# Attention and two MLPs on one core: batch bits, value loads, first issues, clamps and output stores rearranged

## The chip, the cores and the metric

The kernel runs on 1 core of one Trainium2 chip. The metric is device time in microseconds (us), the median of several runs. One execution was also taken by the hardware profiler; its rows are quoted below. Engine names are those of the profile: PE is TensorE's matmul, PEld its weight load, DVE VectorE, ACT ScalarE, POOL GpSimd, SP SyncE; SPq and ACTq are the instructions by which SyncE and ScalarE issue DMAs.

## The reference, cut to what matters

```python
# q, k, v: (4, 8, 768, 48) float32; beta: (4, 8, 768); w_in (384, 2048) and w_out (2048, 384) twice, float64
k_n = k / (norm(k) + 1e-6)
for t in range(768):                                   # per batch b and head h
    y[:, :, t] = einsum('bhd,bhde->bhe', q[:, :, t], state)
    v_old = einsum('bhde,bhd->bhe', state, k_n[:, :, t])
    state += beta_t * einsum('bhd,bhe->bhde', k_n[:, :, t], v[:, :, t] - v_old)
x = y.transpose(0, 2, 1, 3).reshape(3072, 384)
h = x @ w_in;  x = ((a0 + a1 h + a2 h^2 + a3 h^3) / (1 + |b0||h| + |b1|h^2 + 1e-6)) @ w_out   # first MLP
h = x @ w_in2; out = (h * tanh(softplus(h))) @ w_out2                                          # second MLP
```

## The kernel before, in words

**Stages.** The sequence of 768 is cut into 24 steps of 32 positions (`C`), four steps to a group (`GU`), six groups (`NG`). A group is 4 batches x 128 positions = 512 tokens. For each group the attention makes X (512 tokens x 384, kept as a high and a low half), the first MLP turns X into a new X, the second MLP turns that into the output.

**Attention.** The 32 pairs of batch and head lie in four lanes of 32 partitions, eight pairs (`M`) in each. `norms` loads the keys (`load_k`, four DMAs per step) and takes their lengths; `prepare` normalises keys, transposes keys and queries (`load_q`, four DMAs) on TensorE and forms the products within the step; `inverse` solves the triangular systems of four steps at once by 30 pairs of elementwise operations, on GpSimd for groups 1 to 5, on VectorE for group 0; `step` runs the serial recurrence: values (`load_v`, line 239, eight DMAs of 24 KB per step), a swap of key halves between lanes by two DMAs (`swap`), then TensorE, VectorE and ScalarE by turns. In `setup` the first group's keys are loaded by SyncE and ScalarE, beta by eight DMAs of GpSimd.

**Weights.** They arrive as 64-bit floats. `Weights.plan` turns a block of 384 KB into a high and a low 32-bit half in `win` or `wout` and writes it to a scratch `wd` in HBM, from which later groups fetch it. A block passes through: load (`get`, seven DMAs for the first w_in, else one) into one of five `raw` buffers; `clamp` of the upper words (line 624); `fold` or `scale` and `sign`; `shift`; `tail`; `hi`; then the low half, by TensorE and ScalarE (`lo_mm`, `lo_copy`) or by GpSimd (`lo`). The letters of `kind` choose: with "v" the clamp is VectorE's and writes a PSUM bank, and the low half is GpSimd's; without it the clamp is GpSimd's. The first twelve pairs of blocks of the first MLP have no letter; four pairs of the first and four of the second have "v"; the last twelve pairs have "mv".

**MLPs.** A unit (`plan_unit`) is one block of 128 hidden columns for one group: nine matmuls `up` (line 760), activations on ScalarE, VectorE and GpSimd, nine matmuls `down` (line 766) into three output tiles `o0` to `o2`. 16 units make a group of one MLP, 192 units in all. From the second group on the weights of a unit are fetched from `wd` by two DMAs (line 753), into four slots each of `win` and `wout`.

**Output.** For the groups 0 to 4 of the second MLP the result stands by columns: VectorE transposes each tile into one of two buffers `ev` (line 832) and SyncE stores it by 16 DMAs of 16 KB (`store`, line 839), 48 per group. For the last group `down_rows` (line 775) gives rows of tokens in four tiles (`o0` to `o2`, `t0`), which are copied to `ev` (line 818) and stored by one DMA of 192 KB each (`store_rows`, line 847).

**What sets the order.** All work is recorded in a `Plan`: `add` takes an engine, a duration in ns, what is read and written, a due time and `early`; `dma` the same for a DMA, with the time that its issue takes on its queue. `order` works from these numbers which instruction each engine takes next: among those ready, the one with the least time to its due time, less `early`. `lead` gives `early` for attention work: for group 1 `NEAR`, 20 us. The result is a fixed order on each engine; SyncE, ScalarE, VectorE and GpSimd each take theirs strictly in turn. `run` also puts filler matmuls (`heat`, line 909) where the plan sees TensorE idle in the start up.

## Time and profile before

| | us |
|---|---|
| three runs | 1224.94, 1228.59, 1234.18; median 1228.59 |
| profiled execution, device time | 1236.0 |
| its span, first to last instruction | 1234.3 |
| mean granted clock of TensorE in it | 0.941 of 2.4 GHz |

The span is what the rows count, from 0 at the first instruction. The profiled execution is one run among the others, a little longer than their median.

### The profile page before, as it was taken

How to read it: one execution, taken by the hardware profiler on the slowest of the kernel's cores; microseconds unless marked ns; L12 is line 12 of the kernel's file. 1: busy time of each engine (PE TensorE's matmuls, PEld its weight loads, DVE VectorE, ACT ScalarE, POOL GpSimd, SP SyncE). 2: the span in 40 equal slices, each digit the busy share in tenths (PEclk: the TensorE clock that was granted, in tenths of full speed). 3: DMA queues.
4: the chain of work that ended last, by engine and by line, in shares of the span. 5: the costliest groups of instructions: out<-in, count | busy, mean ns of one | idle time of the engine just before them, and what ended most of it. 6: DMA issues, size and time to landing. Idle time of an engine off the chain costs nothing.

```text
span 1234.3 us, 32780 instructions
## 1 busy us (share of the span) xinstructions
PE 1070.5 (87%) x13510; PEld 855.5 (69%) x13510; DVE 654.6 (53%) x1088; ACT 617.3 (50%) x1087; POOL 553.5 (45%) x705
## 2 busy tenths in 40 slices
PE   5566799688878997999899998999986999999885
PEld 4444577466656786777778776887865788788775
DVE  4663389867657742248662357732263578721211
ACT  3334488734367751257752276832263588832211
POOL 5102169695236796726576035683043257600000
PEclk9877889898989998999999999999998999999988
DMA  5575683656763864464866565755536366767462
GB/s 126 121 204 134 211 249 123 208 185 194 218 181 89 251 178 117 117 173 109 234 172 172 128 169 133 227 160 145 154 95 185 94 175 188 190 184 193 121 200 62
DMA packets 201221, 202.80 MB, mean 164 GB/s; under 512 B 133968, under 2 KB 146768, under 8 KB 201072
## 3 DMA queue, kind: packets, MB, share of 16 engines
q1 hardware_dynamic: 198640, 200.22, 58.6%
q8 instruction: 106, 1.74, 0.6%
q10 hardware_dynamic: 2176, 0.39, 0.2%
q14 instruction: 43, 0.35, 0.1%
q0 software_dynamic: 256, 0.10, 0.0%
HBM read 168.40 MB, written 29.88 MB: 161 GB/s over the span
## 4 chain that ended last, share of the span: by engine, by line
PE 54%; SPq 15%; DMA 9%; DVE 7%; POOL 7%; ACT 5%; issue 3%; DVEq 0%; POOLq 0%; ACTq 0%
PE b_h L760 23%; PE b_o L766 20%; SPq L839 7%; DMA kn<-in_k_dram 3%; POOL xs L425 2%; PE b_t L531 2%; POOL tmp L419 2%; SPq L229 2%; PE b_t L510 2%; DMA wout<-wd 1%; PE b_o L775 1%; SPq L617 1%; PE b_t L496 1%; DMA wd<-x 1%; SPq L242 1%
## 5 line engine op out<-in xcount | busy, mean ns | idle before, releaser
L760 PE MATMUL b_h<-x,win 128*128 128x512 f32 x1620 | 416.8, 404 | 32.2 <-DMA win<-wd 14.2
L766 PE MATMUL b_o<-gh,wout 128*128 128x512 f32 x1476 | 378.1, 403 | 18.4 <-DMA wout<-wd 9.6
L760 PEld LDWEIGHTS b_h<-x,win 128*128 128x128 f32 x1620 | 306.7, 193 | 104.1 <-DVE ms L800 15.5
L766 PEld LDWEIGHTS b_o<-gh,wout 128*128 128x128 f32 x1476 | 279.2, 192 | 83.0 <-DMA wout<-wd 9.9
L811 DVE TENSOR_TENSOR gh<-mq,gh 128x512 fp32r<-128x512 f32 x96 | 75.6, 788 | 195.3 <-ACT mq L810 185.1
L798 POOL TENSOR_TENSOR mq<-mq,mr 128x512 f32<-128x512 f32 x96 | 124.1, 1292 | 110.0 <-ACT mr L796 104.4
L809 ACT ACTIVATE gh<-b_h 128x512 fp32r<-128x512 f32 x96 | 57.3, 597 | 214.2 <-PE b_h L760 207.9
L807 POOL TENSOR_TENSOR gh<-mq,gh 128x512 fp32r<-128x512 f32 x96 | 124.0, 1292 | 70.1 <-ACT gh L806 70.0
L799 DVE TENSOR_TENSOR ms<-ms,b_h 128x512 f32<-128x512 f32 x96 | 65.5, 682 | 59.1 <-ACT ms L797 56.9
L425 POOL TENSOR_TENSOR xs<-xs,tmp 128x30 f32<-128x30 f32 (+9 forms) x150 | 84.1, 561 | 11.8
L792 ACT ACTIVATE mq<-b_h 128x512 f32<-128x512 f32 x96 | 56.8, 592 | 62.3 <-PE b_h L760 60.3
L803 DVE SCALAR_TENSOR_TENSOR mq<-mq,b_r 128x512 f32<-128x512 f32 x96 | 65.6, 683 | 38.1 <-ACT b_r L802 34.7
L419 POOL TENSOR_TENSOR tmp<-xs 128x30 f32<-128x30 f32 (+9 forms) x150 | 79.1, 527 | 10.1
L797 ACT ACTIVATE ms<-b_h,ab 128x512 f32<-128x512 f32 x96 | 73.8, 769 | 8.5 <-PE b_h L760 8.1
L790 ACT ACTIVATE mr<-mq,cst 128x512 f32<-128x512 f32 x96 | 69.1, 720 | 16.8 <-POOL mq L798 16.6
L800 DVE SCALAR_TENSOR_TENSOR ms<-ms,ab,b_h 128x512 f32<-128x512 f32 x96 | 71.8, 748 | 3.2
L806 ACT CAST gh<-mq 128x512 fp32r<-128x512 f32 x96 | 58.9, 615 | 27.8 <-DVE mq L805 26.4
L804 DVE SCALAR_TENSOR_TENSOR b_r<-ms,ab,b_r 128x512 f32<-128x512 f32 x96 | 71.9, 749 | 0.0
L805 DVE SCALAR_TENSOR_TENSOR mq<-mq,b_r 128x512 f32<-128x512 f32 x96 | 65.8, 685 | 2.6
L794 POOL TENSOR_SCALAR mr<-mq,ab 128x512 f32<-128x512 f32 x48 | 37.1, 772 | 60.1 <-ACT mq L792 60.1
L802 ACT ACTIVATE b_r<-mr 128x512 f32<-128x512 f32 x96 | 57.7, 601 | 7.5 <-DVE mq L805 6.3
L810 ACT ACTIVATE mq<-b_h 128x512 f32<-128x512 f32 x96 | 56.9, 594 | 2.4 <-PE b_h L760 2.4
(168 smaller groups left out, 1311.4 us busy)
## 6 DMA issues: line engine op xcount, KB each, us to landing
win<-wd SPq DMA_DIRECT2D x164, 384.0 KB
wout<-wd SPq DMA_DIRECT2D x164, 384.0 KB
arena<-in_moe_w_out_dram SPq DMA_DIRECT2D x32, 384.0 KB
wd<-x SPq DMA_DIRECT2D x24, 384.0 KB
wd<-win SPq DMA_DIRECT2D x16, 384.0 KB
wd<-wout SPq DMA_DIRECT2D x16, 384.0 KB
arena<-in_moe_w_in_dram SPq DMA_DIRECT2D x16, 384.0 KB
v<-in_v_dram SPq DMA_DIRECT2D x192, 24.0 KB
```

The lines of the kernel that those rows point to most:

```text
L419: eng.tensor_tensor(out=tv, in0=row[:, j, j + 1:C].unsqueeze(1).to_broadcast([128, j, n]), in1=xs[:, 0:j, j:j + 1].to_broadcast([128, j, n ...
L425: eng.tensor_tensor(out=xs[:, 0:j, j + 1:C], in0=xs[:, 0:j, j + 1:C], in1=tv, op=ALU.add)
L760: nc.tensor.matmul(out=h, lhsT=win[:, a, j], rhs=x[:, c, slab[j]], start=n == 0, stop=n == 8)
L766: nc.tensor.matmul(out=self.banks[f"o{d}"], lhsT=wout[:, a, d], rhs=gh[:, c], start=first and j == 0, stop=last and j == 2,)
L790: act(out=r, in_=q, func=ACTF.Ln, bias=k["c"])
L797: p.add("ACT", 775, lambda: act(out=s, in_=h, func=ACTF.Identity, scale=k["a3"], bias=k["a2"]), [hb], [sb])
L798: p.add("POOL", 1335, lambda: P.tensor_tensor(out=q, in0=q, in1=r, op=ALU.mult), [rb], [qb])
L800: p.add("DVE", 750, lambda: V.scalar_tensor_tensor(out=s, in0=s, scalar=k["a1"], in1=h, op0=ALU.add, op1=ALU.mult), [hb], [sb])
L804: p.add("DVE", 750, lambda: V.scalar_tensor_tensor(out=rp, in0=s, scalar=k["a0"], in1=rp, op0=ALU.add, op1=ALU.mult), [sb], ["r"])
L807: p.add("POOL", 1320, lambda: P.tensor_tensor(out=gh[:, 1], in0=q, in1=gh[:, 0].bitcast(F32), op=ALU.subtract), [qb], [ghb])
L811: p.add("DVE", 755, lambda: V.tensor_tensor(out=gh[:, 1], in0=q, in1=gh[:, 0].bitcast(F32), op=ALU.subtract), [qb], [ghb])
L839: self.nc.sync.dma_start(out=self.out[row:row + 32, d * 128:(d + 1) * 128].rearrange("t (a c) -> a t c", c=32), in_=ev[:, 32 * n:32 * n + 32],
```

## The change

- **Lanes.** Lane e of the keys and queries held the batch 2 (e // 2) + e % 2; now it holds 2 (e % 2) + e // 2. The eight pairs of a lane's values and of beta then lie evenly in HBM, so that `load_v` needs four DMAs of 48 KB instead of eight of 24, and beta four. The rows of the output are permuted back in `store` and `store_rows`.
- **Issues.** In group 0 the queries and values are issued by ScalarE instead of SyncE.
- **Clamps.** All clamps are on GpSimd, in SBUF; the letter "v" becomes "p", which now chooses the low half on GpSimd alone.
- **Output.** Group 4 also uses `down_rows`. Each row tile is stored by four DMAs of 48 KB, tiles 0 and 2 by SyncE, 1 and 3 by ScalarE. There are three `ev` buffers, and `ms0` serves as a fourth. The stores of the groups 0 to 3 are due 20 `PACE` (84 us) after their unit instead of 7.5.
- **Numbers of the planner.** `NEAR` is 40 us; most durations given to the plan are new, so that the order of instructions changes on every engine.

```diff
-NEAR = 20000
+NEAR = 40000
...
-        vv = v.rearrange("b h s d -> (b h) s d").rearrange("(a c n r) s d -> r c a s n d", a=2, c=2, r=2)
+        vv = v.rearrange("b h s d -> (b h) s d").rearrange("(a m r) s d -> r a s m d", a=2, r=2)
-        self.kv = [kv[e // 2, e % 2] for e in range(4)]
+        self.kv = [kv[e % 2, e // 2] for e in range(4)]
-        self.vv = [[vv[1 - e // 2, e % 2, a] for a in range(2)] for e in range(4)]
+        self.vv = [vv[1 - e // 2, e % 2] for e in range(4)]
...
-    def load_v(self, u):
+    def load_v(self, u, engine=None):
         for e in range(4):
-            for a in range(2):
-                self.nc.sync.dma_start(
-                    out=self.v[u % self.NV][32 * e:32 * e + 32, 4 * a:4 * a + 4], in_=self.vv[e][a][C * u:C * u + C]
-                )
+            (engine or self.nc.sync).dma_start(out=self.v[u % self.NV][32 * e:32 * e + 32], in_=self.vv[e][C * u:C * u + C])
...
-            p.dma(4 * 450, 300, lambda: self.load_q(u), (), [qnb], early=lead(AHEADP, G))
+            p.dma(2250, 300, lambda: self.load_q(u, None if G else nc.scalar), (), [qnb], early=lead(AHEADP, G), engine="SP" if G else "ACT")
...
-        p.dma(8 * 400, 300, lambda: self.load_v(u), (), [vb], early=lead(AHEAD, G))
+        p.dma(2250, 300, lambda: self.load_v(u, None if G else nc.scalar), (), [vb], early=lead(AHEAD, G), engine="SP" if G else "ACT")
...
         def clamp():
-            (nc.vector if "v" in kind else nc.gpsimd).tensor_scalar(
-                out=at, in0=high.bitcast(F32), scalar1=self.MOST, scalar2=-self.MOST, op0=ALU.min, op1=ALU.max,
+            nc.gpsimd.tensor_scalar(
+                out=v, in0=high.bitcast(F32), scalar1=self.MOST, scalar2=-self.MOST, op0=ALU.min, op1=ALU.max,
             )
...
-        p.dma(380 if side or self.n else 2500, 384, get, (), [rawb])
-        if "v" in kind:
-            p.add("DVE", 520, clamp, [rawb], [here])
-        else:
-            p.add("POOL", 1490, clamp, [rawb], [here])
+        p.dma(430 if side or self.n else 3300, 384, get, (), [rawb])
+        p.add("POOL", 540, clamp, [rawb], [mb])
...
-        if m == 2 and G == NG - 1:
+        if m == 2 and G >= NG - 2:
...
-                ev, evb = self.ev[b_ % 2], f"ev{b_ % 2}"
+                ev, evb = (self.ev[b_], f"ev{b_}") if b_ < 3 else (self.s[0], "ms0")
...
-                p.dma(340, 200, lambda b_=b_, ev=ev: self.store_rows(G, b_, ev), [evb], ())
+                for c in range(self.B):
+                    eng = "ACT" if b_ % 2 else "SP"
+                    p.dma(500, 50, lambda b_=b_, ev=ev, c=c, eng=eng: self.store_rows(G, b_, ev, c, A if eng == "ACT" else nc.sync), [evb], (), engine=eng)
...
-                ev, evb = self.ev[d % 2], f"ev{d % 2}"
+                ev, evb = self.ev[d], f"ev{d}"
...
-                    p.dma(340, 40, lambda n=n, d=d, ev=ev: self.store(G, d, ev, n), [evb], (), due=due + (LAG + 4) * PACE)
+                    p.dma(590, 40, lambda n=n, d=d, ev=ev: self.store(G, d, ev, n), [evb], (), due=due + 20 * PACE)
...
-    def store_rows(self, G, b, ev):
-        row = (G * GU + b) * C
-        out = self.out.rearrange("(b s) d -> b s d", b=self.B)
-        self.nc.sync.dma_start(out=out[:, row:row + C], in_=ev[:, 0:384])
+    def store_rows(self, G, j, ev, b, engine):
+        row = (b % 2 * 2 + b // 2) * self.S + (G * GU + j) * C
+        engine.dma_start(out=self.out[row:row + C], in_=ev[32 * b:32 * b + 32, 0:384])
```

The order of the instructions, at three places. First SyncE's queue in the start up, behind the loads of the third block of w_in; `v` are values, `qn` queries, `kn` keys, `kns` swapped keys, `arena` the raw weights. Before:

```order
L621 DMA arena<-in_moe_w_in_dram 48x128
L610 DMA arena<-in_moe_w_out_dram 128x384
L242 DMA v_150<-in_v_dram 32x4x48 x8
L610 DMA arena<-in_moe_w_out_dram 128x384
L235 DMA qn_148<-in_q_dram 32x8x48 x4
L477 DMA kns_152<-kn_147 64x4x48
L478 DMA kns_152<-kn_147 64x4x48
L242 DMA v_151<-in_v_dram 32x4x48 x8
```

and in the changed kernel:

```order
L616 DMA arena<-in_moe_w_in_dram 48x128
L605 DMA arena<-in_moe_w_out_dram 128x384
L229 DMA kn_148<-in_k_dram 32x8x48 x4
L605 DMA arena<-in_moe_w_out_dram 128x384
L229 DMA kn_148<-in_k_dram 32x8x48 x4
L612 DMA arena<-in_moe_w_in_dram 48x2x128 x2
L612 DMA arena<-in_moe_w_in_dram 32x2x128
L615 DMA arena<-in_moe_w_in_dram 16x128
L616 DMA arena<-in_moe_w_in_dram 48x128
```

The values and queries are gone from here; the keys of group 1 and the loads of the next weights stand in their place. ScalarE's order at its start, in the changed kernel, where `sq` and `r` are the squares of the keys, and the kernel before has the same squares and no values or queries:

```order
L229 DMA kn_148<-in_k_dram 32x8x48 x8
L892 ACTIVATE minus<-ident_144 128x128
L241 DMA v_151<-in_v_dram 32x8x48 x4
L235 DMA qn_149<-in_q_dram 32x8x48 x4
L303 ACTIVATE sq_171<-kn_148 128x384
L303 ACTIVATE r_170<-kn_148 128x384
L241 DMA v_152<-in_v_dram 32x8x48 x4
L303 ACTIVATE sq_171<-kn_148 128x384
L303 ACTIVATE r_170<-kn_148 128x384
L624 ACTIVATE arena<-arena 128x384
L235 DMA qn_150<-in_q_dram 32x8x48 x4
```

Twelve of the moved issues stand before the last two squares, four more behind them. Second, SyncE's queue at the stores of the fourth group of the second MLP (`out_dram`), among the fetches of weights (`win`, `wout` from `wd`). Before:

```order
L753 DMA win_116<-wd_5_65 128x768
L753 DMA wout_122<-wd_3_63 128x768
L839 DMA out_dram<-ev_138 4x32x32 x16
L839 DMA out_dram<-ev_139 4x32x32 x16
L839 DMA out_dram<-ev_138 4x32x32 x16
L753 DMA win_117<-wd_6_66 128x768
L753 DMA wout_119<-wd_4_64 128x768
L753 DMA win_118<-wd_7_67 128x768
```

and in the changed kernel:

```order
L744 DMA win_117<-wd_6_66 128x768
L832 DMA out_dram<-ev_138 4x32x32 x7
L744 DMA wout_119<-wd_4_64 128x768
L832 DMA out_dram<-ev_138 4x32x32 x2
L744 DMA win_118<-wd_7_67 128x768
L832 DMA out_dram<-ev_138 4x32x32 x4
L744 DMA win_115<-wd_8_68 128x768
L832 DMA out_dram<-ev_138 4x32x32 x3
L744 DMA wout_120<-wd_5_65 128x768
L241 DMA v_151<-in_v_dram 32x8x48 x4
```

The 48 stores stood in one run; now they stand two to seven at a time between single fetches, and the values of a later step among them. Third, GpSimd among the first units of the first MLP: `mq` and `gh` are products and low halves of the units, `x` the low half of a weight block, `mr` a polynomial. Before:

```order
L794 TENSOR_SCALAR mr_130<-mq_126,ab 128x512
L798 TENSOR_TENSOR mq_126<-mq_126,mr_130 128x512
L807 TENSOR_TENSOR gh_134<-mq_124,gh_134 128x512
L798 TENSOR_TENSOR mq_123<-mq_123,mr_131 128x512
L807 TENSOR_TENSOR gh_135<-mq_125,gh_135 128x512
L382 TENSOR_TENSOR mb_164<-beta_t_146,mask_144 128x256
L653 TENSOR_TENSOR x_113<-arena,x_113 128x384
L794 TENSOR_SCALAR mr_132<-mq_124,ab 128x512
L807 TENSOR_TENSOR gh_136<-mq_126,gh_136 128x512
L798 TENSOR_TENSOR mq_124<-mq_124,mr_132 128x512
L653 TENSOR_TENSOR x_113<-arena,x_113 128x384
```

and in the changed kernel:

```order
L373 TENSOR_TENSOR kn_148<-kn_148,nrm_4_187 128x8x48 x3
L785 TENSOR_SCALAR mr_130<-mq_126,ab 128x512
L789 TENSOR_TENSOR mq_126<-mq_126,mr_130 128x512
L798 TENSOR_TENSOR gh_134<-mq_124,gh_134 128x512
L789 TENSOR_TENSOR mq_123<-mq_123,mr_131 128x512
L648 TENSOR_TENSOR x_113<-arena,x_113 128x384
L798 TENSOR_TENSOR gh_135<-mq_125,gh_135 128x512
L619 TENSOR_SCALAR arena<-arena 128x384
L785 TENSOR_SCALAR mr_132<-mq_124,ab 128x512
L789 TENSOR_TENSOR mq_124<-mq_124,mr_132 128x512
L798 TENSOR_TENSOR gh_136<-mq_126,gh_136 128x512
```

A clamp (`arena<-arena`) now stands between the units' instructions, ahead of the product of `mq_124`; before, no clamp stood among the units on this engine.

## Rows read from the trace of the kernel before

**Rows 1.** the page, busy time, share of the span and instructions of TensorE.

```profile
PE 1070.5 (87%) x13510; PEld 855.5 (69%) x13510; DVE 654.6 (53%) x1088; ACT 617.3 (50%) x1087; POOL 553.5 (45%) x705
```

**Rows 2.** stretches: length, busy time by engine, granted clock, DMA share, GB/s.

```profile
0.80:82.50 81.70, 46.49 (x851) 36.62 (x852) 51.30 (x124) 28.15 (x61) 21.24 (x47) 0.81 0.59 147
82.50:157.10 74.60, 48.33 (x1278) 34.86 (x1277) 29.60 (x59) 34.30 (x76) 13.52 (x19) 0.81 0.63 179
157.10:238.00 80.90, 74.56 (x495) 58.86 (x495) 73.82 (x125) 66.46 (x117) 60.63 (x58) 0.96 0.62 186
238.00:290.00 52.00, 37.81 (x194) 29.65 (x195) 36.67 (x61) 21.47 (x42) 47.86 (x78) 0.80 0.61 197
290.00:367.00 77.00, 64.37 (x1487) 50.04 (x1486) 50.95 (x93) 39.28 (x73) 20.25 (x20) 0.93 0.69 201
400.00:440.00 40.00, 37.08 (x308) 29.29 (x296) 31.43 (x49) 30.29 (x51) 29.77 (x38) 1.00 0.83 240
```

**Rows 3.** SyncE's queue in order of time, start up: start, us, issues.

```profile
18.22 4.22 SPq L242 DMA_DIRECT2D v<-in_v_dram  x8
...
22.96 1.92 SPq L235 DMA_DIRECT2D qn<-in_q_dram  x4
...
26.34 5.00 SPq L242 DMA_DIRECT2D v<-in_v_dram  x8
```

**Rows 4.** the chain that ended last, start up: start, us, what.

```profile
46.25 3.08 DMA qn<-in_q_dram
```

**Rows 5.** VectorE in order of time, the first inverse.

```profile
52.02 0.35 DVE L419 TENSOR_TENSOR tmp<-xs,b_o 128x184 f32<-128x184 f32 x1 [5.50 <-ACT xs L433]
```

**Rows 6.** line 242, SyncE's issues of values: duration ns min/median/max.

```profile
L242 SPq DMA_DIRECT2D v<-in_v_dram x40: 311/430/1613, 18.2 to 144.4; - x40
```

**Rows 7.** line 229, ScalarE's issues of keys: duration ns min/median/max.

```profile
L229 ACTq DMA_DIRECT2D kn<-in_k_dram x8: 317/436/472, 0.8 to 6.1; - x8
```

**Rows 8.** waits of TensorE: total us, times, longest.

```profile
PE b_h L760 <- DMA win<-wd: 14.2, 3, 8.3
...
PE b_o L766 <- DMA wout<-wd: 9.6, 4, 3.6
...
PE b_o L766 <- DVE ev L832: 4.6, 2, 2.7
...
PE b_o L775 <- DVE ev L832: 3.2, 1, 3.2
```

**Rows 9.** TensorE in order of time, two units right behind a wait.

```profile
936.73 4.18 PE L760 MATMUL b_h<-x,win 128*128 128x512 f32 x9 [8.28 <-DMA win<-wd]
...
1183.09 4.11 PE L760 MATMUL b_h<-x,win 128*128 128x512 f32 x9 [5.43 <-DMA win<-wd]
```

**Rows 10.** SyncE's queue, stores of the fourth group.

```profile
905.23 28.05 SPq L839 DMA_DIRECT2D out_dram<-ev  x48
```

**Rows 11.** clamps (line 624): busy us, mean ns, idle before by releaser.

```profile
L624 DVE TENSOR_SCALAR b_r<-arena 128x384 f32<-128x384 f32 x24 | 13.4, 560 | 0.7
...
L624 POOL TENSOR_SCALAR arena<-arena 128x384 f32<-128x384 f32 x24 | 12.9, 537 | 93.7 <-PE b_h L658 28.8 <-DMA kn<-in_k_dram 23.9 <-DMA arena<-in_moe_w_in_dram 17.7
...
L624 DVE TENSOR_SCALAR b_t<-arena 128x384 f32<-128x384 f32 x16 | 8.9, 559 | 8.0 <-DMA arena<-in_moe_w_in_dram 7.7
```

**Rows 12.** clamps on GpSimd: duration ns min/median/max, first and last start.

```profile
L624 POOL TENSOR_SCALAR arena<-arena x24: 518/528/713, 12.3 to 131.3; 128x384 f32<-128x384 f32 x24
```

**Rows 13.** TensorE, two units with column results and two with row results.

```profile
1140.24 2.20 PE L760 MATMUL b_h<-x,win 128*128 128x512 f32 x9
...
1144.32 2.20 PE L760 MATMUL b_h<-x,win 128*128 128x512 f32 x9
...
1189.12 2.24 PE L760 MATMUL b_h<-x,win 128*128 128x512 f32 x9
...
1193.31 2.24 PE L760 MATMUL b_h<-x,win 128*128 128x512 f32 x9
```

**Rows 14.** SyncE's queue, the last four stores.

```profile
1220.74 7.72 SPq L847 DMA_DIRECT2D out_dram<-ev  x4
```

71 lines of the change are left out of this document (34 added, 37 removed).

## The prediction

> **What bounds the kernel now.** I read the page first: TensorE is busy 87% of the span [rows 1], so nothing that TensorE hides is worth anything, and what can be won is the other 164 us (1234.3 - 1070.5) and the time that it ran at its lower clock. Then the stretches [rows 2], which show three regimes. Up to 157 us TensorE does set-up work, 46.5 of 81.7 us and 48.3 of 74.6, at a mean granted clock of 0.81, that is, part of the time at 1.2 GHz instead of 2.4. From 157 to 367 us it shares the time with the conversion of the second weights. From 400 us on it is nearly always busy. So I looked for what it waits for in each, in the list of waits, SyncE's queue and the chain.
>
> In the start up, SyncE is the late one. Its queue issues without a pause, and values, queries, values are issued one behind the other for 4.22 + 1.92 + 5.00 us [rows 3], all of which the chain lists, while the weight loads that the conversions wait for stand behind them. Then a query load, issued late, is on the chain for another 3.08 us [rows 4]; TensorE and ScalarE wait for it in their order, and VectorE's inverse stands still for 5.50 us because ScalarE has not reached the copy that it needs [rows 5].
>
> Later the waits of TensorE have one origin. At the end of a group of the second MLP, SyncE issues 48 stores, in the fourth group all in one row: 28.05 us [rows 10], 0.58 each, and the fetches of weights stand behind them. TensorE waits for fetched weights 14.2 + 9.6 us in seven places and for the two output tiles to be free 4.6 + 3.2 us in three [rows 8]. Right behind such a wait a unit's nine matmuls take 4.18 or 4.11 us [rows 9], against 2.04 in a steady unit (half of the 4.08 from one start to the next, 1144.32 - 1140.24 [rows 13]): the lower clock costs about 2 us per wait, in four places about 8.
>
> **The change part by part.** The sums are made against the profiled execution's own time, 1236.0 us (span 1234.3 and 1.7 around it). It lies 0.6% above the median of the three runs, 1228.59; at the end I scale by 1228.59 / 1236.0 = 0.994.
>
> *Start up.* 16 query issues and 16 value issues of the first group move to ScalarE's queue, and 16 more value issues disappear (32 become 16). That is 48 issues off SyncE. An issue has a median of 0.43 us [rows 6], 0.48 with the gap behind it (5.00 + 4.22 + 1.92 us for 20 [rows 3] are 0.56, with waits in them), so 23 us. On the chain I find 11.1 us of them [rows 3] and the pause of 5.5 [rows 5], 16.6. Against it: ScalarE pays 0.44 per issue [rows 7], and twelve issues stand ahead of the last two squares and four more ahead of the logarithm of the first norms. Part of this hides behind VectorE's reductions; I put the delay of that chain at 3.7 us (eight issues). Net 13. The other 16 issues lie beside ScalarE's slack, 28.2 us busy of 81.7 [rows 2]; each waits for a tile that was read long before in its order. If that cover were gone they would cost 7 us. Bounds: nothing gained (the DMA engines turn out late, or ScalarE gives back what SyncE wins) and 28.5 - 3.7 = 25 us (all 23 and the pause).
>
> On this the trace and a rule of the skill differ. SyncE's issue time is on the chain [rows 3], and the DMA engines are busy 0.59 and 0.63 of these stretches, against 0.83 in a later one [rows 2]. The Trainium skill, DMA: Bandwidth & Descriptors, section Issuing engines are not separate DMA queues, says that issuing from several engines saves only the issuing time, which is usually small beside the transfer. By the rows the term is 13 us, by that rule about none.
>
> *Clamps.* 40 clamps leave VectorE: 24 and 16 of 0.56 us [rows 11], 22.4 us. They go to GpSimd, where 24 like them take 0.537 [rows 11], 21.5 us more there. From 157 to 238 us VectorE is busy 73.8 of 80.9 and GpSimd 60.6; from 238 to 290 GpSimd is the late one, 47.9 of 52 [rows 2], with the inverse of the second group. In the new order four clamps stand inside that inverse, but six low halves instead of ten, at 1 us each: 2 us less. About ten conversions lie ahead of it on the chain, 5.6 us of clamps less on VectorE; 14 clamps more stand ahead on GpSimd, 7.5 us, in a stretch with 20.3 us to spare. I take 4 us gained, between 15 (two thirds of the 22.4) and a loss whose size depends on what a clamp waits for (third rival).
>
> The 24 clamps on GpSimd take 518 to 713 ns, with a median of 528 [rows 12]; with all 40 at the upper end it would be 7 us more, inside GpSimd's spare time. The Trainium skill, SBUF — State Buffer, section SBUF: two separate sides, says that VectorE and GpSimd share a port pair which one instruction holds to its end, so that the other stands. The rows up to 713 ns do not refute that. By that rule the four clamps inside the inverse would each stand for up to a whole VectorE operation of 0.55 us, and the term would be 2 us instead of 4.
>
> *Stores.* The 48 stores of each of the first four groups stay, with a new due time and a real price in the planner. In the new order at most seven follow each other (4.1 us), with fetches between. The queue then needs 48 x 0.58 + 14 fetches and 8 query issues at 0.43 [rows 6], 9.5, = 37 us for seven units, of 4.1 us each without attention work beside them; it falls behind by at most 9 us, and the fetches run four units, 16 us, ahead. The fifth group's 48 become 16, half of them on ScalarE, whose work there is two operations per unit. The third and fourth output tiles remove the waits for a free one. To be had: 14.2 + 9.6 + 4.6 + 3.2 + 8 = 39.6 us; I take 32, since some fetches will still come late. Bounds 0 and 39.6.
>
> *Tail.* The last store is issued at 1220.74 + 7.72 = 1228.5 us [rows 14], 5.8 us before the end. Now eight issues on each queue at 0.48 end near 1225.0 (ScalarE's start at 1221.1). Gain 3.5 at the same landing time; I take 5, because 48 KB land sooner than 192 (3.08 us [rows 4]). Bounds 3 and 8.
>
> *Fifth group by rows.* A unit with row results takes 4.19 us (1193.31 - 1189.12), one with column results 4.08 [rows 13]: 16 x 0.11 = 1.7 us lost. The halved value issues of later groups and of beta lie beside TensorE: nothing, and 3 us if a fetch waited behind them.
>
> Sum: 13 + 4 + 32 + 5 - 1.7 = 52.3. 1236.0 - 52.3 = 1183.7; times 0.994, 1177 us.
>
> **The rivals.**
> 1. The start up is not shortened: the transfers or the serial attention steps are late, not SyncE. For it: DMA shares near 0.6 with waits for landings between the issues [rows 4]. Against it: 0.83 is reached later [rows 2]. 13 us less: 1196.7, scaled 1190. This is also the sum by the skill's rule on issuing engines.
> 2. The stores do not do what the edit says: the queue issues in order, a fetch that waits for TensorE holds the stores behind it, they bunch up, and the fetches are late once more. Without the 32 us: 1215.7, scaled 1208. Against it: the new order lets no more than seven follow each other.
> 3. The other side: GpSimd is held up by late weights. A clamp waits for its raw weights at the head of GpSimd's queue, and products and low halves of the units, which TensorE needs, stand behind it. Price: on VectorE these 40 waited 0.7 + 8.0 us, 0.2 each; the 24 on GpSimd had 93.7 us of idle time before them, 3.9 each [rows 11]. I take the former, the same instructions with the same loads. GpSimd's spare time from 157 to 367 us is 20.3 + 4.1 + 56.8 = 81 us [rows 2]. At 3.9 each the 40 need 40 x 4.4 = 178, 97 over: 1177 + 4 + 97 = 1278. Slower than before from about 2.9 us each.
> 4. The new order, made with new costs everywhere, gives back elsewhere what the edits win: near 1228.
>
> **How the numbers follow.** Forecast 0.58 (own range 1152 to 1192), first rival 0.17, second 0.12, third 0.06, fourth 0.04, something else and slower 0.03. A measurement of this kernel tells about 1%, 12 us, from no change. The first three are faster by more than that: 0.87. Same: 0.05 (the fourth and a part of the other rest). Slower: 0.08 (the third, and what is left). Upper ends of all terms, 25 + 15 + 39.6 + 8 - 1.7 = 86, give 1143; the range starts at 1150, as not all can hold, and ends at 1212, with the second rival in it.
>
> **What would show it.** Right: the dense units of TensorE begin near 144 us instead of 157, where the second stretch of [rows 2] ends; no wait for fetched weights over 2 us at the ends of groups; the last store within 5 us of the last matmul. Wrong: SyncE idle before 150 us with weights landing no sooner (rival 1); fetches late behind stores (rival 2); clamps on GpSimd with long idle times before them between 157 and 290 us, and TensorE idle there for more than the present 20.5 us, 80.9 - 74.6 and 52.0 - 37.8 [rows 2] (rival 3).

## The result and the profile after

| | us |
|---|---|
| the changed kernel, four runs | 1144.19 to 1148.46; median 1147.60 |
| the kernel before, four runs beside it | 1224.94 to 1234.18; median 1228.29 |
| ratio, 95% interval | 0.9333, 0.9292 to 0.9374 |
| profiled execution after: device time, span | 1146.76, 1145.0 |

The change gains 80.7 us where 52 were forecast, and 1147.6 lies 2.4 us below the range. The direction was right; the stores and the tail came out larger than forecast, the start up and the clamps smaller, and one term, the planner's numbers, was missing. The page of the changed kernel, busy times as in [rows 1]:

```profile
PE 1050.4 (92%) x13568; PEld 847.8 (74%) x13568; DVE 630.6 (55%) x1047; ACT 613.7 (54%) x1089; POOL 571.8 (50%) x741
```

Its chain that ended last, in shares by engine, first before, then after:

```profile
PE 54%; SPq 15%; DMA 9%; DVE 7%; POOL 7%; ACT 5%; issue 3%; DVEq 0%; POOLq 0%; ACTq 0%
```

```profile
PE 75%; POOL 8%; DVE 5%; DMA 5%; ACT 3%; issue 3%; SPq 1%; ACTq 0%; DVEq 0%; POOLq 0%
```

SyncE's issuing has left the chain, from 15% to 1%. To see where, both traces have to be cut at the same work, not at the same time. I cut them at the first `up` matmul of the units 0, 16, 32 and 40 (counted in order of time) and at the last matmul. Columns as in [rows 2]; before:

```profile
0.80:137.10 136.30, 83.77 (x2029) 63.41 (x2029) 71.85 (x167) 51.94 (x117) 30.20 (x62) 0.81 0.60 153
137.10:230.00 92.90, 80.18 (x515) 62.69 (x514) 76.32 (x130) 70.98 (x128) 62.39 (x58) 0.93 0.61 187
230.00:357.90 127.90, 98.52 (x1670) 76.62 (x1669) 90.05 (x158) 59.62 (x115) 67.12 (x98) 0.89 0.69 210
357.90:397.00 39.10, 36.39 (x340) 29.00 (x339) 27.36 (x43) 29.82 (x48) 22.72 (x22) 0.96 0.40 95
397.00:1220.60 823.60, 771.59 (x8964) 623.80 (x8963) 388.39 (x592) 404.43 (x682) 370.83 (x464) 0.98 0.59 162
```

and after:

```profile
0.80:117.40 116.60, 78.31 (x1967) 60.80 (x1968) 66.54 (x154) 46.52 (x104) 24.95 (x53) 0.84 0.64 160
117.40:208.80 91.40, 81.82 (x651) 64.42 (x649) 78.47 (x135) 76.56 (x143) 69.69 (x73) 0.98 0.68 207
208.80:329.30 120.50, 94.09 (x1608) 71.98 (x1599) 71.20 (x125) 56.30 (x110) 81.21 (x126) 0.92 0.68 210
329.30:368.60 39.30, 38.44 (x418) 30.94 (x416) 31.62 (x50) 32.53 (x52) 26.14 (x26) 1.00 0.75 196
368.60:1138.60 770.00, 757.78 (x8941) 619.63 (x8939) 382.29 (x587) 401.32 (x680) 369.64 (x462) 1.00 0.64 171
```

The first dense unit comes 19.7 us sooner (137.1 to 117.4), unit 40 28.4 (397.0 to 368.6). The last stretch, dense work with the output of five groups in it, is 53.6 us shorter: TensorE idles in it 52.0 us before (823.6 - 771.59) and 12.2 after, and its matmuls take 13.8 us less, at a granted clock of 1.00 instead of 0.98. Behind the last matmul, in the tail, stand 13.7 us before (1234.3 - 1220.6) and 6.4 after. The parts sum to 89.3 us against 80.7 between the medians, since the profiled execution of before was 7.7 us over the median of 1228.29 and that of after 0.8 under its own; a lead read against the trace of before can be too large by some 8 us.

What TensorE waits for (total us, times, longest). Of before [rows 8] has the waits for weights and for `ev`; two more rows of it, in the last stretch:

```profile
PE b_h L760 <- DVE ms L800: 5.0, 7, 1.1
...
PE b_t L496 <- DVE r L490: 3.0, 3, 1.6
```

and all of the list in the last stretch after:

```profile
PE b_t L349 <- DVE lg L367: 6.8, 1, 6.8
PE b_t L480 <- issue: 1.7, 2, 1.2
PE b_h L751 <- DVE ms L791: 1.1, 2, 0.6
PE b_h L751 <- ACT mq L801: 1.1, 1, 1.1
PE b_o L757 <- DVE ev L825: 0.7, 1, 0.7
PE b_t L492 <- issue: 0.6, 1, 0.6
```

No wait for a fetched weight is left. SyncE's queue at the end of the fourth group, where [rows 10] had 48 stores in one row:

```profile
852.16 0.32 SPq L744 DMA_DIRECT2D win<-wd  x1
852.96 4.15 SPq L832 DMA_DIRECT2D out_dram<-ev  x7
857.22 0.41 SPq L744 DMA_DIRECT2D wout<-wd  x1
857.67 1.12 SPq L832 DMA_DIRECT2D out_dram<-ev  x2
858.89 0.42 SPq L744 DMA_DIRECT2D win<-wd  x1
859.36 2.37 SPq L832 DMA_DIRECT2D out_dram<-ev  x4
861.83 0.76 SPq L744 DMA_DIRECT2D win<-wd  x1
```

At most seven stores stand between two fetches, as the order had shown. I had overlooked one thing in the trace of before: VectorE itself stood for the stores. Line 832 (the transposes into `ev`) from 390 us on, what VectorE sat idle for just before them (us, times):

```profile
L832 DVE STREAM_TRANSPOSE ev<-b_o x12: 674/710/718, 557.9 to 1160.2; 128x512 f32<-128x512 f32 x12
its engine sat idle before it (us, times) until:
  DMA out_dram<-ev: 15.0, 4
```

With two buffers VectorE waited 15.0 us in four places until a store had left one, and the units' operations stood behind it. Line 825 after the change has no such wait, and TensorE's waits for VectorE's `ms` fell from 5.0 us in seven places to 1.1 in two. Only part of the 15.0 us is seen at TensorE: at the ends of the fourth and the fifth group as waits for `ev`, of 1.9 and 3.2 us, which [rows 8] has; behind the other two as a wait for `ms` of 0.8 us each. The first of these, VectorE and then TensorE:

```profile
569.56 0.72 DVE L832 STREAM_TRANSPOSE ev<-b_o 128x512 f32<-128x512 f32 x1 [2.86 <-DMA out_dram<-ev]
```

```profile
574.13 2.11 PE L760 MATMUL b_h<-x,win 128*128 128x512 f32 x8 [0.78 <-DVE ms L800]
```

The tail after, both queues (the last matmul ends at 1138.6):

```profile
1138.68 3.60 SPq L839 DMA_DIRECT2D out_dram<-ev  x8
```

```profile
1138.69 1.81 ACTq L839 DMA_DIRECT2D out_dram<-ev  x4
1140.59 1.80 ACTq L839 DMA_DIRECT2D out_dram<-ms  x4
```

### The profile page after: what moved, and what is told of

It reads as the page before. It is cut to its first block, busy times and chain, and to the rows that moved or that the text cites. A ratio compares the mean times of both kernels' runs of the same rounds, so it can differ in the third digit from the quotient of the medians.

```text
span 1145.0 us, 32730 instructions
## 1 busy us (share of the span) xinstructions
PE 1050.4 (92%) x13568; PEld 847.8 (74%) x13568; DVE 630.6 (55%) x1047; ACT 613.7 (54%) x1089; POOL 571.8 (50%) x741
## 4 chain that ended last, share of the span: by engine, by line
PE 75%; POOL 8%; DVE 5%; DMA 5%; ACT 3%; issue 3%; SPq 1%; ACTq 0%; DVEq 0%; POOLq 0%
PE b_h L751 31%; PE b_o L757 24%; PE b_o L766 4%; PE b_t L527 3%; POOL xs L421 3%; DMA arena<-in_moe_w_in_dram 3%; POOL tmp L415 3%; PE b_t L506 2%; PE b_t L492 2%; PE b_t L361 2%; PE b_t L480 2%; PE b_t L766 1%; PE b_t L349 1%; PE b_h L653 1%; DMA kn<-in_k_dram 1%
## 5 line engine op out<-in xcount | busy, mean ns | idle before, releaser
L751 PE MATMUL b_h<-x,win 128*128 128x512 f32 x1620 | 409.2, 397 | 12.8 <-ACT mq L801 9.7
L751 PEld LDWEIGHTS b_h<-x,win 128*128 128x128 f32 x1620 | 299.1, 189 | 80.3 <-ACT mq L801 10.3
L757 PE MATMUL b_o<-gh,wout 128*128 128x512 f32 x1332 | 335.4, 397 | 5.0 <-POOL wout L648 2.8
L757 PEld LDWEIGHTS b_o<-gh,wout 128*128 128x128 f32 x1332 | 246.2, 189 | 59.7 <-POOL wout L648 3.6
L802 DVE TENSOR_TENSOR gh<-mq,gh 128x512 fp32r<-128x512 f32 x96 | 71.9, 750 | 205.3 <-ACT mq L801 198.1
L619 POOL TENSOR_SCALAR arena<-arena 128x384 f32<-128x384 f32 x64 | 34.0, 533 | 98.5 <-PE b_h L653 58.0
L783 ACT ACTIVATE mq<-b_h 128x512 f32<-128x512 f32 x96 | 56.9, 592 | 41.1 <-PE b_h L751 39.7
L797 ACT CAST gh<-mq 128x512 fp32r<-128x512 f32 x96 | 58.8, 615 | 16.2 <-DVE mq L796 13.1
```

The source lines that it names most:

```text
L751: nc.tensor.matmul(out=h, lhsT=win[:, a, j], rhs=x[:, c, slab[j]], start=n == 0, stop=n == 8)
L757: nc.tensor.matmul(out=self.banks[f"o{d}"], lhsT=wout[:, a, d], rhs=gh[:, c], start=first and j == 0, stop=last and j == 2,)
L802: p.add("DVE", 755, lambda: V.tensor_tensor(out=gh[:, 1], in0=q, in1=gh[:, 0].bitcast(F32), op=ALU.subtract), [qb], [ghb])
```

## The experiments

Each kernel ran beside the kernel before on the same chip; "gain" is the difference of the two medians, and the interval is the ratio's. "Unit 0" and "unit 40" are the starts of these units, "last stretch" goes from unit 40 to the last matmul, "tail" from there to the end; all four are us of the profiled execution. The parts are named as in the change: *issues* (lanes, values and beta by fewer DMAs, first queries and values on ScalarE), *clamps*, *output*, and *numbers* (the planner's new durations and `NEAR`).

| kernel | us | ratio (95%) | gain | unit 0 | unit 40 | last stretch | tail |
|---|---|---|---|---|---|---|---|
| only_out | 1171.66 | 0.9539 (0.9502-0.9575) | 58.4 | 135.9 | 386.5 | 773.8 | 6.4 |
| only_issue | 1226.41 | 0.9968 (0.9944-0.9992) | 3.6 | 141.6 | 400.5 | 814.0 | 10.6 |
| only_clamp | 1236.37 | 1.0057 (1.0029-1.0085) | -6.3 | 129.6 | 402.6 | 817.9 | 13.6 |
| only_price | 1209.68 | 0.9843 (0.9809-0.9877) | 20.4 | 109.0 | 371.2 | 823.0 | 13.5 |
| no_price | 1158.97 | 0.9449 (0.9416-0.9482) | 69.2 | 132.8 | 376.7 | 772.1 | 6.5 |
| no_issue | 1149.15 | 0.9372 (0.9325-0.9418) | 79.1 | 114.1 | 370.3 | 770.8 | 6.4 |
| no_clamp | 1149.03 | 0.9369 (0.9338-0.9400) | 79.2 | 120.3 | 369.4 | 770.6 | 6.9 |
| no_out | 1201.05 | 0.9802 (0.9759-0.9844) | 27.2 | 117.0 | 368.3 | 821.3 | 10.2 |
| out_num | 1178.99 | 0.9602 (0.9568-0.9637) | 48.6 | 132.2 | 389.8 | 772.9 | 13.4 |
| out_rows | 1208.50 | 0.9854 (0.9804-0.9904) | 19.1 | 136.0 | 399.6 | 808.8 | 6.4 |
| pr_dma | 1230.04 | 1.0014 (0.9995-1.0032) | -2.4 | 123.2 | 395.6 | 821.1 | 13.3 |
| pr_pe | 1224.15 | 0.9987 (0.9963-1.0010) | 3.5 | 130.8 | 396.7 | 819.4 | 13.6 |
| pr_near | 1235.98 | 1.0060 (1.0034-1.0086) | -6.5 | 134.7 | 396.1 | 825.2 | 13.7 |
| near_dma | 1215.27 | 0.9890 (0.9864-0.9915) | 14.2 | 122.1 | 379.8 | 821.8 | 14.0 |
| after_near20 | 1157.66 | 0.9417 (0.9390-0.9444) | 71.8 | 117.6 | 375.0 | 775.7 | 6.4 |
| after_sp | 1138.24 | 0.9257 (0.9230-0.9283) | 91.2 | 111.6 | 361.1 | 770.7 | 6.9 |
| only_lanes | 1219.16 | 0.9922 (0.9896-0.9949) | 7.0 | 128.0 | 387.3 | 820.1 | 9.9 |
| sp_clampv | 1142.27 | 0.9303 (0.9275-0.9331) | 83.8 | 108.5 | 359.7 | 770.8 | 6.8 |

### Each part alone, in the kernel before

only_out, the hunks of `ev`, `G >= NG - 2`, `store` and `store_rows`:

```diff
+        self.ev = ring("ev", 3, [128, TOK])
...
+        if m == 2 and G >= NG - 2:
...
+                    p.dma(500, 50, lambda b_=b_, ev=ev, c=c, eng=eng: self.store_rows(G, b_, ev, c, A if eng == "ACT" else nc.sync), [evb], (), engine=eng)
...
+                    p.dma(590, 40, lambda n=n, d=d, ev=ev: self.store(G, d, ev, n), [evb], (), due=due + 20 * PACE)
```

> The kernel before with the output part alone: three ev buffers, stores of the groups 0 to 3 at 590 ns each and due 20 PACE after their unit, groups 4 and 5 by rows with four DMAs per tile on two queues. Theory A (the forecast's terms with the sizes that the two traces give): it brings what was won after the unit at 397 us, 53.6 us up to TensorE's end (39.5 us of idle time and about 17 of lower clock) and 7.2 behind it, so 55 to 62 us, 1167 to 1174 us, and the units before 397 us start as before. Theory B (the new durations of the planner make the better order, the stores were only one of its rows): under 35 us.

only_issue, which with the lanes also needs four store DMAs of 48 KB, on SyncE, for each row tile of the last group:

```diff
+        vv = v.rearrange("b h s d -> (b h) s d").rearrange("(a m r) s d -> r a s m d", a=2, r=2)
...
+            (engine or self.nc.sync).dma_start(out=self.v[u % self.NV][32 * e:32 * e + 32], in_=self.vv[e][C * u:C * u + C])
...
+            p.dma(2250, 300, lambda: self.load_q(u, None if G else nc.scalar), (), [qnb], early=lead(AHEADP, G), engine="SP" if G else "ACT")
...
+        p.dma(2250, 300, lambda: self.load_v(u, None if G else nc.scalar), (), [vb], early=lead(AHEAD, G), engine="SP" if G else "ACT")
```

> The kernel before with the lanes swapped, values by four DMAs, and the first group's queries and values issued by ScalarE; all other durations of the planner as before. Theory A: SyncE's issues were late in the start up; the first dense unit starts 13 to 20 us sooner than 137.1 us, and most of that is kept: 13 to 20 us faster, 1208 to 1215 us. Theory B: the first unit's gain comes from the planner's prices; here under 6 us.

only_clamp:

```diff
-            (nc.vector if "v" in kind else nc.gpsimd).tensor_scalar(
+            nc.gpsimd.tensor_scalar(
...
-        if "v" in kind:
-            p.add("DVE", 520, clamp, [rawb], [here])
-        else:
-            p.add("POOL", 1490, clamp, [rawb], [here])
+        p.add("POOL", 540, clamp, [rawb], [mb])
```

> The kernel before with all clamps on GpSimd at 540 ns. Theory A: 2 to 8 us faster, all of it between 157 and 290 us. Theory B: nothing alone (within 3 us), since SyncE and not VectorE sets the pace of the conversions as long as its queue is as before. Third: slower, if clamps wait for raw weights on GpSimd's queue.

only_price, some twenty numbers, for example:

```diff
-NEAR = 20000
+NEAR = 40000
...
-        p.dma(380 if side or self.n else 2500, 384, get, (), [rawb])
+        p.dma(430 if side or self.n else 3300, 384, get, (), [rawb])
...
-            p.add("POOL", 1490, clamp, [rawb], [here])
+            p.add("POOL", 540, clamp, [rawb], [here])
```

> The kernel before with nothing but the planner's new durations (matmuls, loads, fetches, conversions, the clamps of GpSimd among them) and NEAR at 40 us; the stores keep 340 ns and their due time. No instruction is added or removed. Theory A: little, within 10 us of before, the ends of groups keep their waits for weights. Theory B: 25 us faster or more, with the waits at the ends of groups gone or the start up shortened.

The four gains, 58.4 + 3.6 - 6.3 + 20.4, make 76.1 of the 80.7 us. The output part is as theory A put it, except that unit 40 comes 10.5 us sooner; the first group of the second MLP ends ahead of it, with 3.6 us of VectorE waiting for `ev` at 378 us. The issues gain under 6 us (theory B), and 3.1 of their 3.6 lie in the tail, 10.6 us against 13.7, from the smaller row stores that came with the lanes. The clamps come out as the third theory had it, slower; the price of the 24 clamps that were on GpSimd before went from 1490 to 540 in the same edit, so that the 6.3 us are not the move's alone.

The numbers fall between their two theories, and they are the surprise: no operation of the computation is added or removed, and they give 20.4 us, in the start up (unit 0 at 109.0), where the forecast had put the issues; the issues alone bring unit 0 no sooner. One thing does change with the plan, the number of filler matmuls of `heat` and when they run; in before and in only_price:

```profile
L909 PE MATMUL b_o<-ident,zero x94: 269/332/582, 10.9 to 65.9; 128*128 128x128 f32 x94
```

```profile
L909 PE MATMUL b_o<-ident,zero x112: 270/275/579, 10.9 to 108.1; 128*128 128x128 f32 x112
```

The mean granted clock up to unit 0 is 0.81 before and 0.89 in only_price. Whether the fillers or the order bring that, and how much of the 20.4 us it is, no run separates.

Why the issues alone did not help shows in SyncE's waits in the start up of only_issue:

```profile
SPq L613 <- DVE arena L639: 13.2, 1, 13.2
```

SyncE now ran ahead, had all five raw buffers filled, and stood from 69.8 to 83.0 us, because VectorE was in the first group's inverse, which ended at 80.1 here and at 69.8 before. The bound had passed to the inverse, and the inverse itself was later, as the norms were (24.7 us, 13.0 before).

### Each part taken back, in the changed kernel

The same four sets of hunks, undone one at a time: no_price, no_issue, no_clamp, no_out.

> The changed kernel with the planner's old durations and NEAR at 20 us; issues, clamps and output as changed. Theory A (the parts add up): 20 us slower than the changed kernel, near 1168 us, with the first dense unit 15 to 30 us later. Theory B (they work on each other: with the new issues on ScalarE the old durations do no harm): within 6 us of the changed kernel.

> The changed kernel with the old lanes, values by eight DMAs, and the first group's queries and values issued by SyncE. Theory A (the parts add up): 4 us slower than the changed kernel, 1150 to 1153 us. Theory B (the issues were worth the forecast's 13 us, and the kernel with this part alone hid it, because its old durations stood against it): 10 to 15 us slower, 1158 to 1163 us.

> The changed kernel with the clamps of 40 conversions back on VectorE, writing a PSUM bank. Theory A (the parts add up): 6 us faster than the changed kernel, near 1142 us. Theory B (in the new order VectorE is the late engine of the conversions): 3 to 8 us slower, 1151 to 1156 us.

> The changed kernel with the old output: two ev buffers, stores at 340 ns and due 7.5 PACE after their unit, only the last group by rows, one DMA per pair of tile and batch on SyncE alone. Theory A (the parts add up): 58 us slower, near 1206 us, the ends of groups wait for fetched weights 30 us or more and the granted clock falls there again. Theory B (the durations of loads and fetches alone bring the fetches forward): under 40 us slower.

By the ratios, against 0.9333, and 1228 us: the output is worth 58 us (theory A), the numbers 14 (between the two theories), and issues and clamps (0.0039 and 0.0036, 4 to 5 us) are not told from nothing; for the issues theory B falls, for the clamps theory A. So the size of the output holds up in both surroundings and that of the numbers roughly, while the clamps' loss doesn't come back. Two things make the parts less clean than they look: no_out keeps four store DMAs per row tile, so its tail is 10.2 us and not 13.7, and the clamp's price of 540 belongs to only_price but isn't taken back in no_price. The last stretch is the clearest: in the ten kernels with the old output, before among them, it took 814 to 825 us; in the nine with new stores 770 to 776. Between the two bands lies out_rows below (808.8), part of the output too. No other edit moves it out of them.

### Inside the output

out_num takes three `ev` buffers, 590 ns and the late due time; out_rows takes the rest of the part.

```diff
-        self.ev = ring("ev", 2, [128, TOK])
+        self.ev = ring("ev", 3, [128, TOK])
...
-                ev, evb = self.ev[d % 2], f"ev{d % 2}"
+                ev, evb = self.ev[d], f"ev{d}"
...
-                    p.dma(340, 40, lambda n=n, d=d, ev=ev: self.store(G, d, ev, n), [evb], (), due=due + (LAG + 4) * PACE)
+                    p.dma(590, 40, lambda n=n, d=d, ev=ev: self.store(G, d, ev, n), [evb], (), due=due + 20 * PACE)
```

> Of the output part only the stores of the column groups: three ev buffers, 590 ns each in the plan, due 20 PACE after their unit. Rows, queues and DMA sizes of the last groups as before. Theory A (fetches stand behind stores in SyncE's order, and every wait costs its length and the lower clock behind it): most of the output part's 58 us, 40 to 50 us faster than before, 1180 to 1190 us, with no wait for fetched weights over 2 us after 400 us. Theory B (the number of stores is what counts, and the third buffer and the due time only move the waits): under 25 us.

```diff
-        if m == 2 and G == NG - 1:
+        if m == 2 and G >= NG - 2:
...
-                p.dma(340, 200, lambda b_=b_, ev=ev: self.store_rows(G, b_, ev), [evb], ())
+                for c in range(self.B):
+                    eng = "ACT" if b_ % 2 else "SP"
...
```

> Of the output part only the last two groups: rows for the fifth group too, four DMAs per row tile on two queues, three ev buffers and ms0 for these tiles; the stores of the groups 0 to 3 as before. Theory A: 10 to 20 us faster than before (the waits at the end of the fifth group, 8.6 us with about 3 of lower clock, and 7 behind the last matmul, less 1.7 for units by rows), 1210 to 1220 us. Theory B (the number of stores counts): 25 us or more.

Theory A both times. With all 240 column stores still there, the buffer and the order alone give 48.6 us; what each of the two gives no run separates. No wait for a fetched weight or for `ev` is left in the list of out_num. The last stretch of out_num in one row (770.0 us and 757.78 in the changed kernel):

```profile
389.80:1162.70 772.90, 756.67 (x8972) 616.50 (x8970) 386.86 (x592) 404.74 (x682) 367.76 (x464) 1.00 0.62 170
```

The rows keep the waits at the ends of the groups before the fifth, here in out_rows:

```profile
PE b_h L760 <- DMA win<-wd: 8.4, 1, 8.4
...
PE b_o L766 <- DMA wout<-wd: 7.6, 2, 4.0
```

The two parts overlap by 9 us (48.6 + 19.1 against 58.4): either removes the waits at the end of the fifth group. The tail falls from 13.7 us to about 10 by the smaller DMAs (only_issue and only_lanes have them on SyncE alone) and to 6.4 by the second queue.

### Which of the numbers

pr_dma has those of DMA issues, pr_pe those of TensorE:

```diff
-            p.dma(4 * 450, 300, lambda: self.load_q(u), (), [qnb], early=lead(AHEADP, G))
+            p.dma(2250, 300, lambda: self.load_q(u), (), [qnb], early=lead(AHEADP, G))
...
-        p.dma(380 if side or self.n else 2500, 384, get, (), [rawb])
+        p.dma(430 if side or self.n else 3300, 384, get, (), [rawb])
...
```

> Of the planner's new numbers only those of DMA issues: key and query loads 2250, the first blocks of w_in 3300, other blocks, scratch writes 430, fetches 370, swaps 1350. Theory A (SyncE's queue is what the start up is short of, and the planner has to know its price): the greater part of the 20 us that all the new numbers gave, 12 us or more, and the first group's inverse ends near 60 us instead of 70. Theory B (the durations of TensorE make the order): under 6 us here, and the next kernel has the gain.

```diff
-            p.add("PE", 600, transpose(kn, tk), [knb], [tk], early=lead(AHEADP, G))
+            p.add("PE", 500, transpose(kn, tk), [knb], [tk], early=lead(AHEADP, G))
...
-        p.add("PE", 890, x_mm, [yb], [bx], early=lead(AHEAD, G))
+        p.add("PE", 740, x_mm, [yb], [bx], early=lead(AHEAD, G))
...
```

> Of the planner's new numbers only those of TensorE (transposes 500, products 980, 780, 760, 1560, 740, low halves 750). Theory A: under 6 us. Theory B: the greater part of the 20 us, 12 us or more.

Neither gives anything, so the greater part of the 20 us is in neither alone. But pr_dma does bring unit 0 13.9 us sooner (123.2) and the first inverse's end to 61.5 us, and then loses it: it reaches unit 24 at 287.7 us, 1.4 before the kernel before does. There the second group's inverse runs on GpSimd. Its first operation of 30, by kernel, starts (us): 238.0 before, 245.8 in pr_dma, 251.9 in only_clamp, 257.5 in only_issue, but 208.2 in only_price and 213.2 in the changed kernel; it takes some 40 us in each. So theory C: the start up's gain is kept if `NEAR` brings this inverse ahead too. only_price and the changed kernel have `NEAR` at 40 us.

```diff
-NEAR = 20000
+NEAR = 40000
```

> The kernel before with NEAR at 40 us and nothing else. Theory C: between the first dense unit and 400 us the second group's inverse on GpSimd is the bound (in the kernels with issues, clamps or DMA durations alone it ran from about 238 to 285 us or later, and the lead of the first unit was lost there); NEAR alone moves it ahead, and with the start up as before that gives 5 to 15 us. Theory D (NEAR plays no part, the gain of the new numbers came from the conversions' durations on GpSimd): within 4 us of before.

near_dma is pr_near and pr_dma together, after_near20 the changed kernel with `NEAR` back.

> The kernel before with NEAR at 40 us and the planner's new numbers of DMA issues. Theory C: the two together have what neither has alone, the first unit near 123 us by the DMA numbers and a second inverse that begins near 210 us: 15 to 22 us faster than before. Theory D: under 6 us, as the DMA numbers alone (none).

> The changed kernel with NEAR back at 20 us. Theory C: the second group's inverse begins 15 to 30 us later, and most of what the new numbers gave is lost: 10 to 16 us slower than the changed kernel, 1158 to 1164 us. Theory D: within 4 us of the changed kernel.

`NEAR` alone costs 6.5 us, where theory C had 5 to 15 gained: the second inverse begins at 231.3 us, 6.7 sooner than before, and unit 40 only 0.9 sooner. The DMA numbers alone give nothing, the two together give 14.2 (theory C: 15 to 22), and without `NEAR` the changed kernel loses 10 (0.0084 of 1228). Line 419 on GpSimd (ns min/median/max, first to last start) in pr_dma and in near_dma:

```profile
L419 POOL TENSOR_TENSOR tmp<-xs x30: 253/536/905, 245.8 to 284.1; 128x30 f32<-128x30 f32 x2, 128x58 f32<-128x58 f32 x2, 128x84 f32<-128x84 f32 x2, 128x108 f32<-128x108 f32 x2
```

```profile
L419 POOL TENSOR_TENSOR tmp<-xs x30: 235/532/1059, 214.9 to 256.1; 128x30 f32<-128x30 f32 x2, 128x58 f32<-128x58 f32 x2, 128x84 f32<-128x84 f32 x2, 128x108 f32<-128x108 f32 x2
```

So the two work together as theory C says, with the sizes a little below it, but why `NEAR` alone costs time it doesn't say. It is not the whole rule either: after_near20 reaches unit 40 at 375.0, 22 us before the kernel before does, with its second inverse at 239.1. What else holds the conversions between 200 and 330 us stays open; so does what the durations of conversions and clamps add to the pair (14.2 of 20.4). The fillers go the same way as the start up here too: 118 of them in pr_dma and near_dma, with a mean granted clock up to unit 0 of 0.88 and 0.91; but only_lanes has 78, at 0.83, and its unit 0 comes 9.1 us sooner than before, so they are not all of it.

### Who issues

after_sp is the changed kernel with the first queries and values on SyncE; the lanes and the four DMAs stay.

```diff
-            p.dma(2250, 300, lambda: self.load_q(u, None if G else nc.scalar), (), [qnb], early=lead(AHEADP, G), engine="SP" if G else "ACT")
+            p.dma(2250, 300, lambda: self.load_q(u), (), [qnb], early=lead(AHEADP, G))
...
-        p.dma(2250, 300, lambda: self.load_v(u, None if G else nc.scalar), (), [vb], early=lead(AHEAD, G), engine="SP" if G else "ACT")
+        p.dma(2250, 300, lambda: self.load_v(u), (), [vb], early=lead(AHEAD, G))
```

> The changed kernel with the first group's queries and values issued by SyncE again; lanes and four DMAs per step of values stay. Theory E (ScalarE pays for the issues: the first fold and the first inverse wait behind them, the first conversion ends at 24 us instead of 17): the first inverse begins near 34 us instead of 43.5, and the time is the same or up to 6 us better than the changed kernel. The forecast's first term: 10 us slower or more.

It is the best kernel of the study: 1138.24 us, and its interval (0.9230 to 0.9283) lies below that of the changed kernel (0.9292 to 0.9374). It is 9.4 us below the changed kernel by the medians, 6.3 by the profiled spans. ScalarE's queue shows why. The changed kernel, start, us, idle before and its releaser:

```profile
8.57 4.29 ACTq L241 DMA_DIRECT2D v<-in_v_dram  x4
13.54 2.90 ACTq L235 DMA_DIRECT2D qn<-in_q_dram  x4
16.49 0.52 ACT L303 ACTIVATE sq<-kn 128x384 f32<-128x384 f32 x1 [9.03 <-DMA arena<-in_moe_w_in_dram]
...
18.85 2.81 ACTq L241 DMA_DIRECT2D v<-in_v_dram  x4
...
23.60 1.41 ACTq L235 DMA_DIRECT2D qn<-in_q_dram  x3
25.05 0.23 ACT L315 ACTIVATE nrm<-nrm 128x32 f32<-128x32 f32 x1 [2.00 <-DMA kn<-in_k_dram]
```

and after_sp:

```profile
10.12 0.51 ACT L303 ACTIVATE sq<-kn 128x384 f32<-128x384 f32 x1
...
13.31 0.23 ACT L315 ACTIVATE nrm<-nrm 128x32 f32<-128x32 f32 x1 [1.08 <-DVE nrm L309]
```

Sixteen issues stand ahead of the first norms (`nrm`): with the one query issue left out of the rows, 0.32 us, they take 4.29 + 2.90 + 2.81 + 1.41 + 0.32 = 11.73 us, 0.73 each, and the norms come 11.7 us later. The kernel before shows the same without the new numbers: its norms come at 13.0 us, with the issues on ScalarE (only_issue) at 24.7, with the fewer issues on SyncE (only_lanes below) at 13.4. The first inverse then begins at 43.5 us instead of 33.2 and ends at 72.5 instead of 58.8. Some of the other sixteen issues cost too: in the changed kernel four query issues hold ScalarE ahead of a weight's `fold`, VectorE waits for that, and the copy of `xs` that the inverse needs stands two instructions further on ScalarE, at 48.15 us:

```profile
47.36 0.52 ACT L624 ACTIVATE arena<-arena 128x384 f32<-128x384 f32 x1 [4.32 <-DMA mq<-in_q_dram]
```

```profile
47.92 0.56 DVE L633 TENSOR_SCALAR b_r<-arena 128x384 int32<-128x384 int32 x1 [1.91 <-ACT arena L624]
```

The last two kernels: only_lanes, the fewer issues without ScalarE, in the kernel before, with four store DMAs per row tile as in only_issue; and sp_clampv, after_sp with the 40 clamps back on VectorE.

```diff
-        p.dma(8 * 400, 300, lambda: self.load_v(u), (), [vb], early=lead(AHEAD, G))
+        p.dma(4 * 400, 300, lambda: self.load_v(u), (), [vb], early=lead(AHEAD, G))
```

> The kernel before with the lanes swapped and the values by four DMAs, all issued by SyncE (values 1600 ns per step in the plan); nothing else. Theory E (fewer issues help, moving them to ScalarE hurts by some 9 us, and the two gave 4 together): 8 to 13 us faster than before, 1216 to 1221 us. Theory F (without an earlier second inverse a shorter start up is lost by 400 us, as with the DMA numbers alone): within 4 us of before, although the first dense unit starts 8 us sooner or more.

> The changed kernel with the first group's queries and values on SyncE and the 40 clamps back on VectorE. If the clamps on GpSimd cost in the new order what they cost in the old (6 us), about 1132 us; if they gain the forecast's 4 us, about 1142 us; beside the 1138.2 us of the same kernel with all clamps on GpSimd.

only_lanes gains 7.0 us by the medians, 9.6 by the ratio: nearer to theory E. But 3.8 of that is the tail, 9.9 us against 13.7, from the smaller row stores, so the fewer value and beta issues gain 3 to 6. With ScalarE's issues on top the whole was 3.6. That it keeps 10 us at unit 40 (part of which can be the trace of before, 7.7 us over the median) with a second inverse as late as 246.9 is the other thing that theory C doesn't explain. sp_clampv is 4.0 us above after_sp by the medians, with intervals that overlap, while its profiled span (1137.2 us) is 1.5 below (1138.7): in the new order the sign of the clamps stays open, and it is small. In the old order they cost 6.3, together with their new price in the plan, with the second inverse starting 13.9 us later on GpSimd.

## Why the prediction was wrong, point by point

Two steps of the sum failed, and they more than make up the 28.4 us between 52.3 and 80.7: the output was sized too small, by some 23 us, most of it the stores, and the planner's numbers, 14 to 20, were put at nothing without a reason. Two more terms, the start up and the clamps, were too large and took part of it back.

- **Stores: the mechanism right, the size wrong; this is the first step that failed.** "To be had: 14.2 + 9.6 + 4.6 + 3.2 + 8 = 39.6 us; I take 32", with 39.6 as an upper bound, was no bound. out_num alone gained 48.6. Three things were mis-sized. The idle time won in the last stretch is 39.8 us, not 31.6. Waits for fetched weights and for `ev` are 28.7 of it (29.4 us before, 0.7 after; 2.7 of the forecast's 31.6 lie ahead of unit 40). The other 11.1 are waits that I did not count as the stores': 3.9 for `ms`, 3.0 for `r`, the rest smaller ones. Of these, 0.8 us stand right behind a wait of VectorE for `ev` in each of two places; whether the others came with the stores or with the new order is not shown, but in out_num, too, the idle time falls by 35.8 us. The lower clock was priced at 8 us for four waits; the last stretch shows 13.8. And the 20% kept back for late fetches was not needed: none is late.
- **Fifth group and tail.** The tail's 5 (bounds 3 to 8) became 7.3. The form of the working was right: about half comes with the smaller DMAs, half with the second queue. Units by rows take 4.19 us in the changed kernel too, as the forecast's 1.7 had it. Output as a whole, 32 - 1.7 + 5 = 35.3 forecast, 58 measured.
- **The planner's numbers: no term at all, the second step that failed.** The forecast gave the new order a rival (the fourth) that could only take away. It gave 14 to 20 us: in only_price unit 0 comes 28 us sooner, and unit 40 still 26. By which numbers is shown in part only (DMA issues and `NEAR` together 14.2); why stays open, and the fillers with their higher clock are a rival that no run tested.
- **Start up: 13 forecast, none to 5 measured.** The issues on the chain [rows 3] were a real cost: fewer of them gain 3 to 6. "I put the delay of that chain at 3.7 us (eight issues)" is what failed here. The forecast knew of the sixteen ahead of the norms and took half as hidden (eight at its 0.44 us are 3.5); nothing was hidden, and with the pauses between them they take 0.73 us each, 11.7 in all. The price could have been read from [rows 7]: 0.44 is what an issue lasts, but the eight start between 0.8 and 6.1 us, 0.76 apart. The first rival had the right size (none) for this part; the runs point to ScalarE, and not to late DMA engines. The Trainium skill, DMA: Bandwidth & Descriptors, section Issuing engines are not separate DMA queues, says that issuing from several engines saves only the issuing time. Its rule gave about none for this term, and the runs agree on that size. They go further: what was saved on SyncE was paid on ScalarE, and the kernel with SyncE issuing is 9 us faster (1147.60 and 1138.24).
- **Clamps: 4 forecast.** In the kernel before they cost 6.3, with their new price in the plan; in the changed one they are not told from nothing. The third rival's idle time ahead of the clamps is there; the page's group of them after, idle time before them and its releasers:

```profile
L619 POOL TENSOR_SCALAR arena<-arena 128x384 f32<-128x384 f32 x64 | 34.0, 533 | 98.5 <-PE b_h L653 58.0 <-DMA arena<-in_moe_w_in_dram 13.6 <-DMA arena<-in_moe_w_out_dram 11.9
```

  But the 24 clamps of before already had 93.7 before them [rows 11]; with 40 more the sum rose by 4.8 only, about 0.1 each, near the 0.2 that I had taken, and a clamp lasts 533 ns, as the 537 before. (By its own terms that rival turns slower from about 2.7 us each, not 2.9.) TensorE idles from unit 0 to unit 32 for 36.0 us, against 42.1.
- **The signs named ahead.** The unit that began at 157.1 us begins at 133.8 (forecast 144). No fetched weight is late by 2 us. The last store has been issued 3.8 us behind the last matmul (1140.59 + 1.80 and 1138.6).

The sum again with what was measured: output 58, numbers 14 to 20, issues none to 5, clamps between -6 and 4. The ends give 66 and 87, with 80.7 between them; so wide a sum confirms little beyond the output.

## What to carry to other kernels

Ask of each store in a shared queue both what stands behind it there and which engine waits for its buffer: here VectorE stood 15.0 us for it, and TensorE's waits show that in part as `ev` and in part under another name, `ms`. A list scheduler's durations are part of a change like any edit: look in the traces at the places where the serial work (here two inverses) starts. And an issue moved to a computing engine holds up everything that stands behind it in that engine's order: price it by the distance from one issue's start to the next, not by how long one lasts.
